# Eight adjacent output rows, zero-padded stationary slices, one store and filler matmuls in a decode kernel

## The chip, the cores and the metric

The kernel runs on one core of a Trainium2 chip. The metric is the device time of one execution in microseconds (us), given as the median of several executions. The profile's span is about 2 us shorter than that time (before: 110.88 us of span in an execution of 112.67 us), so differences are compared within one kind, never across. Engines are PE (matrix multiply), PEld (its weight loads), DVE (vector), ACT (scalar), POOL and SP. Most of the loads, and one store of the kernel before, are issued by SP; a few by ACT.

## The reference, cut to what matters

One token per batch row (2 rows, D = 448) is normalized. It goes through an attention over the last 2048 cache positions (16 query heads, 8 cached heads, head size 256) and the output product with wo, and separately through a two-layer block with w1 and w2. The two results are multiplied and added to x:

```python
xn = _layernorm(x, axis=-1)
s = _A_ref(xn, A_k_cache, A_v_cache, A_wq, A_wo)     # (2,1,4096) @ wo (4096,448) at its end
g = _silu(_B_ref(xn, B_w1, B_w2))                     # relu(xn@w1) @ w2 (1792,448)
return x + s * g
```

## The kernel before

44.11 MB of cache and weights are loaded for an output of 2 x 448 numbers. The attention is cut into four units u (batch x half of the cached heads). For each, K is transposed on PE, scores, softmax and the product with V follow. Apart from the load of x, the change touches only the end: the w2 product (`do_F`), the turn of the attention result into stationary form (`at2`, the operand that the weight loads bring into PE), the wo product and the store; around the last values product (`do_PV(3)`) it adds matmuls. wo arrives in five loads of 12, 12, 4, 2 and 2 row blocks of 128 rows each.

Both end products are held as four column groups i of 112 columns. Each matmul of a group of four writes its own 32-column strip of the PE array (`tile_position=(0, 32*i)`), so row b of group i stands in partition 32*i + b: eight useful rows, spread over 128 partitions.

```python
# x, loaded in the same layout (4 rows, 32 partitions apart, for each b)
d_xc = [pr.dma(ACTE, view(x_c, 0, [[1, NCOL]], n=4, p0=b, pstep=32),
               A_x[b, 0, :].rearrange("(i n) -> i n", i=4), [p_xc]) for b in range(B)]
...
# do_F: the w2 product; 14 row blocks x 4 column groups
for f in range(14):
    for i in range(4):
        lo = W2_AT + f * D + i * NCOL
        o = pr.op(PE, mm(view(fbk, 0, [[1, NCOL]], n=B, p0=32 * i), h_sb[:, 2 * f:2 * f + 2],
                         w2_sb[:, lo:lo + NCOL], f == 0, f == 13, tile_position=(0, 32 * i)), deps)
...  # exp, add, reciprocal, multiply: g_sb, 128 x 112
# the end of the program
do_F()
do_PV(3)
attend_scale(3)
attend_turn(3)
for b in range(2):
    ...  # two small matmuls and copies: at2, 128 x 64
for j in range(32):
    deps = deps + [landed.get(j)]            # the load that brought row block j
    for i in range(4):
        lo = j * D + i * NCOL
        m_o = pr.op(PE, mm(obk[32 * i:32 * i + B, 0:NCOL], at2[:, 2 * j:2 * j + 2],
                           wo_sb[:, lo:lo + NCOL], j == 0, j == 31, tile_position=(0, 32 * i)), deps)
        deps = []
v_t = ...   # tmp = obk * g_sb       128 x 112
v_o = ...   # out_sb = tmp + x_c     128 x 112
d_o = [pr.dma((SP, ACTE)[b], out[b, 0, :].rearrange("(i n) -> i n", i=4),
              view(out_sb, 0, [[1, NCOL]], n=4, p0=b, pstep=32), [v_o]) for b in range(B)]
```

## Time and profile before

| | before |
|---|---|
| median of executions | 112.84 us (112.78 to 112.84) |
| span of the profiled execution | 110.88 us |
| last wo load landed | 107.46 us |
| last wo matmul ended | 107.86 us |
| last vector operation ended | 108.49 us |
| from there to the end (the "tail" below) | 2.39 us |

These are rows of the page of the kernel before. The first three cut the span in 40 slices of 2.77 us: tenths of PE's time, tenths of full clock that PE was granted, tenths of the DMA engines' time. (The trace's record of the clock begins at 19.24 us; the nines before that are no measurement.) The last is the chain of waits, followed back from the last instruction, by engine.

```profile
PE   0010299995428999859999949699985464293480
PEclk9999999999995589995899995799999985555555
DMA  3988979898899889889989998998999999999920
...
DMA 56%; PE 34%; DVE 4%; SPq 2%; issue 1%; ACT 1%
```

The DMA row is full almost to the end, and the chain is mostly loads: the kernel is bound by bringing in its bytes. The end of the chain, in order of time (start, us, what), says what remains after the last byte.

```profile
83.07 24.39 DMA kbuf<-in_A_wo_dram
107.46 0.04 issue
107.50 0.39 PE obk L265 x8
...
107.91 0.28 DVE tmp L513
...
108.22 0.27 DVE out_sb L515
```

PE waits for the last load, does only the last eight of 128 wo matmuls after it, and two vector operations follow. The timeline of the kernel before shows how the wo matmuls run and how the stores are issued (start, duration, engine, line, operation, count).

```profile
102.38 1.29 PE L265 MATMUL obk<-kbuf,at 128*2 128x112 bf16 x48 [0.29 <-DVE at L502]
...
108.22 0.27 DVE L515 TENSOR_TENSOR out_sb<-tmp,x_c 128x112 bf16<-128x112 f32 x1
108.52 0.66 SPq L36 DMA_DIRECT2D out_dram<-out_sb  x1
108.52 0.56 ACTq L36 DMA_DIRECT2D out_dram<-out_sb  x1
```

48 matmuls in 1.29 us are 27 ns each, although PE runs at half clock. In the trace, the four of a row block start 1 to 6 ns apart, mostly 3 or 4, and the next four 93 ns later: four at a time, as the Trainium skill ("TensorE: Matmul & The Clock Gate", Part 3) says of tiles in different column groups.

The windows view of the kernel before, cut on the grid of the clock's changes (window, its length, then PE busy, PEld, DVE, ACT, POOL, clock, DMA share, GB/s), shows where the clock fell and how busy PE was then.

```profile
87.50:90.92 3.42, 2.11 (x70) 1.52 (x62) 1.51 (x5) 0.00 (x0) 0.00 (x0) 1.00 1.07 461
90.92:94.33 3.41, 1.55 (x64) 1.24 (x56) 1.26 (x3) 0.26 (x1) 0.00 (x0) 0.50 0.91 392
94.33:97.74 3.41, 1.39 (x16) 0.55 (x20) 0.27 (x1) 0.00 (x0) 0.00 (x0) 0.50 1.00 414
97.74:101.16 3.42, 2.47 (x28) 0.57 (x16) 0.81 (x2) 0.00 (x0) 0.00 (x0) 0.50 1.02 430
```

After a window in which PE was busy 2.11 of 3.42 us, the clock fell, and none of the later windows, of up to 2.47 busy us, was followed by a rise. The changes of the clock lie multiples of 3.41 us apart in the whole trace, which agrees with Part 1 of the same page: a free-running window of about 3.4 us.

### The profile page before, as it was taken

To read this page: it belongs to the slowest core of one execution; us is meant where nothing else is said; L and a number is where in the kernel's file an instruction comes from. 1 tells how busy PE (TensorE), PEld (TensorE's weight loads), DVE (VectorE), ACT (ScalarE), POOL (GpSimd) and SP (SyncE) were. 2 spreads that over 40 slices of the span, in tenths; PEclk is the share of its full clock that TensorE was granted. 3 is DMA by queue.
4 is the path that set the end of the run, shared out by engine and by line. 5 is a ranking of instruction groups with operands and counts; after the bars stand their busy time and mean duration, and the time that the engine had idled before them with its cause. 6 is when DMAs were issued, how large, how long until landed. Compare 5 with 4: busy or idle time off the path is not lost.

```text
span 110.9 us, 1921 instructions
## 1 busy us (share of the span) xinstructions
PE 74.0 (67%) x845; PEld 49.7 (45%) x845; DVE 48.0 (43%) x110; ACT 35.4 (32%) x43; POOL 1.9 (2%) x11
## 2 busy tenths in 40 slices
PE   0010299995428999859999949699985464293480
PEld 0000299952127977413777513397632244022350
DVE  2182042953433356553775653477546333104001
ACT  1960036760020647602286602076820200000000
POOL 6000000000000000000000000000000000000000
PEclk9999999999995589995899995799999985555555
DMA  3988979898899889889989998998999999999920
GB/s 95 473 379 379 520 331 496 355 567 372 378 532 414 378 378 556 384 378 532 417 366 390 526 402 378 520 426 378 387 382 416 454 434 423 408 426 427 394 98 1
DMA packets 2619, 44.22 MB, mean 399 GB/s; under 512 B 306, under 2 KB 564, under 8 KB 948
## 3 DMA queue, kind: packets, MB, share of 16 engines
q1 hardware_dynamic: 2584, 44.11, 93.5%
q8 instruction: 6, 0.10, 0.3%
q10 hardware_dynamic: 28, 0.00, 0.0%
q14 instruction: 1, 0.01, 0.0%
HBM read 44.11 MB, written 0.00 MB: 398 GB/s over the span
## 4 chain that ended last, share of the span: by engine, by line
DMA 56%; PE 34%; DVE 4%; SPq 2%; issue 1%; ACT 1%
DMA kbuf<-in_A_k_cache_dram 34%; PE tb L285 25%; DMA kbuf<-in_A_wo_dram 22%; PE sbk L265 5%; PE obk L265 2%; SPq L36 2%; PE mbk L265 1%; DVE s_sb L335 1%; ACT e_sb L340 1%; DVE rm L318 1%; DVE q_n L399 1%; PE mbk L345 1%; DVE pt L350 0%; DVE qz L409 0%; PE mbk L403 0%
## 5 line engine op out<-in xcount | busy, mean ns | idle before, releaser
L285 PE MATMUL tb<-ident_f,kbuf 128*128 128x128 f32 x256 | 36.6, 306 | 6.3 <-DMA kbuf<-in_A_k_cache_dram 6.3
L285 PEld LDWEIGHTS tb<-ident_f,kbuf 128*128 128x128 f32 x256 | 33.5, 161 | 10.4 <-DMA kbuf<-in_A_k_cache_dram 6.4
L295 ACT ACTIVATE kt<-tb 128x1024 bf16<-128x1024 bf16 x28 | 27.4, 1023 | 26.2 <-PE tb L285 26.2
L293 DVE COPY kt<-tb 128x1024 bf16<-128x1024 bf16 x36 | 24.7, 690 | 21.7 <-PE tb L285 21.7
L265 PE MATMUL obk<-vbuf,pt 128*16 128x512 bf16 x128 | 13.5, 529 | 3.5 <-DMA vbuf<-in_A_v_cache_dram 3.5
L265 PE MATMUL sbk<-kt,qz 128*32 128x512 bf16 x128 | 11.0, 393 | 1.7 <-DVE kt L293 1.1
L340 ACT ACTIVATE e_sb<-s_sb 128x512 bf16<-128x512 f32 x4 | 2.5, 630 | 22.9 <-DVE s_sb L335 22.9
L265 PEld LDWEIGHTS obk<-vbuf,pt 128*16 128x16 bf16 x128 | 3.2, 101 | 8.2 <-DMA vbuf<-in_A_v_cache_dram 4.4
L265 PE MATMUL mbk<-ident,xg 2*128 2x2 bf16 x7 | 0.3, 163 | 7.4 <-DVE xg L237 7.4
L372 DVE TENSOR_SCALAR o_sb<-obk,rs 128x512 bf16<-128x512 f32 x4 | 2.9, 735 | 5.4 <-PE obk L265 5.4
L265 PEld LDWEIGHTS sbk<-kt,qz 128*32 128x32 bf16 x128 | 2.7, 94 | 5.5 <-DVE kt L293 2.1
L265 PE MATMUL obk<-kbuf,at 128*2 128x112 bf16 x128 | 3.7, 292 | 2.1 <-DMA kbuf<-in_A_wo_dram 1.8
L318 DVE TENSOR_REDUCE rm<-sbk 128x4 f32<-128x512 f32 x4 | 2.8, 691 | 4.3 <-PE sbk L265 4.3
L350 DVE COPY pt<-mbk 128x512 bf16<-128x512 bf16 x4 | 1.7, 424 | 5.6 <-PE mbk L345 5.6
L345 PE MATMUL mbk<-ident,e_sb 128*128 128x128 bf16 x16 | 2.2, 286 | 2.6 <-ACT e_sb L340 2.6
L265 PEld LDWEIGHTS obk<-kbuf,at 128*2 128x2 bf16 x128 | 2.6, 112 | 3.1 <-DMA kbuf<-in_A_wo_dram 2.6
L265 PEld LDWEIGHTS mbk<-ident,xg 2*128 2x128 bf16 x7 | 0.3, 101 | 7.4 <-DVE xg L237 7.4
L345 PEld LDWEIGHTS mbk<-ident,e_sb 128*128 128x128 bf16 x16 | 1.3, 122 | 5.0 <-ACT e_sb L340 5.0
L323 PE MATMUL mbk<-ident_f,rm 128*1 128x128 f32 x4 | 1.1, 270 | 3.4 <-DVE rm L321 3.4
L265 PE MATMUL mbk<-one_f,mall 1*128 1x1 f32 x8 | 1.6, 268 | 2.5 <-DVE mall L330 2.5
L335 DVE SCALAR_TENSOR_TENSOR s_sb<-sbk,bias,low 128x512 f32<-128x512 f32 x4 | 3.0, 751 | 0.1
L323 PEld LDWEIGHTS mbk<-ident_f,rm 128*1 128x1 f32 x4 | 0.3, 79 | 5.4 <-DVE rm L321 5.4
(68 smaller groups left out, 37.0 us busy)
## 6 DMA issues: line engine op xcount, KB each, us to landing
kbuf<-in_A_k_cache_dram SPq DMA_DIRECT2D x4, 4096.0 KB, 27.1
vbuf<-in_A_v_cache_dram SPq DMA_DIRECT2D x3, 4096.0 KB, 37.0
vbuf<-in_A_wq_dram SPq DMA_DIRECT2D x1, 3584.0 KB, 20.1
kbuf<-in_B_w_dram SPq DMA_DIRECT2D x2, 1568.0 KB, 23.6
vbuf<-in_A_v_cache_dram SPq DMA_DIRECT2D x1, 3072.0 KB, 25.8
kbuf<-in_A_wo_dram SPq DMA_DIRECT2D x2, 1344.0 KB, 22.2
vbuf<-in_A_v_cache_dram SPq DMA_DIRECT2D x1, 1024.0 KB, 27.7
kbuf<-in_A_wo_dram SPq DMA_DIRECT2D x1, 448.0 KB, 24.3
```

What stands on the lines that cost most here:

```text
L36: o = _Op(eng, lambda e: e.dma_start(dst, src), [d for d in deps if d is not None], True)
L265: return lambda e: e.matmul(out_ap, lhsT=lhsT, rhs=rhs, start=start, stop=stop, skip_group_check=True, **kw)
L285: o = pr.op(PE, lambda e, n=n, lo=lo: e.matmul(bank_f[:, n * 128:(n + 1) * 128], lhsT=src_f[:, lo:lo + 128], rhs=ident_f[:, :], start=True ...
L293: evac[n_th] = pr.op(DVE, lambda e: e.tensor_copy(dst[:, :], bank[:, :]), deps)
L295: evac[n_th] = pr.op(ACTE, lambda e: e.activation(dst[:, :], bank[:, :], ACT.Copy), deps)
L318: v = pr.op(DVE, lambda e: e.tensor_reduce(out=rm4[:, :], in_=view(sbk, 0, [[1, 4], [4, 128]]), axis=AX.X, op=ALU.max), [st["S", u]])
L323: m = st["rmT", u] = pr.op(PE, lambda e: e.matmul(mbk_ap(0, 128, 1), lhsT=rm[:, :], rhs=ident_f[:, :], start=True, stop=True, is_transpose ...
L335: v = st["shift", u] = pr.op(DVE, lambda e: e.scalar_tensor_tensor(out=view(s_sb, 0, [[4, 128], [1, 4]]), in0=view(sbk, 0, [[4, 128], [1, ...
L340: a = st["exp", u] = pr.op(ACTE, lambda e: e.activation(e_sb[:, :], s_sb[:, :], ACT.Exp, accum_out=ssum[:, 0:1]), [v, st.get(("Pt", u - 1) ...
L345: o = pr.op(PE, lambda e, j=j: e.matmul(mb16[:, 512 + 128 * j:640 + 128 * j], lhsT=e_sb[:, 128 * j:128 * j + 128], rhs=ident[:, :], start= ...
L350: v = st["pt", u] = pr.op(DVE, lambda e: e.tensor_copy(view(pt[u % 2], 0, [[256, 2], [16, 16], [8, 2], [1, 8]]), view(mb16, 512, [[256, 2] ...
L372: st["osb", u] = st["obk"] = pr.op(DVE, lambda e: e.tensor_scalar(out=o_sb[:, :], in0=obk[:, :], scalar1=rs[:, u:u + 1], scalar2=None, op0 ...
```

## The change

The eight useful rows of the output, of the gate and of x are to stand in eight adjacent partitions (row 4*b + i), so that one store suffices. All four matmuls of a row block now write the same eight rows. To make matmul i touch only rows i and 4 + i, its stationary operand is an eight-column slice, out of an array with two useful columns and zeros around them (11 columns per row block, slice shifted by i). The sums of the other rows get zeros added. Matmuls without use ("fillers", four, two and one of 512 columns) are to keep PE's clock up. The whole diff:

```diff
--- before.py
+++ after.py
@@ -105,6 +105,8 @@
     FC = DFF // 2
     WO_PARTS = [12, 12, 4, 2, 2]
     NCOL = D // 4
+    NROW = 4 * B
+    GAP = NROW + 3
     NTB = 5
     ON_ACT = (1, 3, 5, 8, 10, 12, 14)
     FAR = -1.0e30
@@ -146,12 +148,12 @@
         q_n = named("q_n", [128, 512], BF)
         qz = named("qz", [128, 2 * NU * 64], BF)
         h_n = named("h_n", [128, FC // 4], BF)
-        h_sb = named("h_sb", [128, 28], BF)
-        x_c = named("x_c", [128, NCOL], BF)
-        ea = named("ea", [128, NCOL], F32)
-        g_sb = named("g_sb", [128, NCOL], F32)
-        tmp = named("tmp", [128, NCOL], F32)
-        out_sb = named("out_sb", [128, NCOL], BF)
+        h_z = named("h_z", [128, 14 * GAP], BF)
+        x_c = named("x_c", [NROW, NCOL], BF)
+        ea = named("ea", [NROW, NCOL], F32)
+        g_sb = named("g_sb", [NROW, NCOL], F32)
+        tmp = named("tmp", [NROW, NCOL], F32)
+        out_sb = named("out_sb", [NROW, NCOL], BF)
         rm4 = named("rm4", [128, 4], F32)
         rmm = named("rmm", [128, 4], F32)
         rm = named("rm", [128, 1], F32)
@@ -165,7 +167,7 @@
         pt = [named(f"pt{i}", [128, 512], BF) for i in range(2)]
         o_sb = named("o_sb", [128, 512], BF)
         at_exp = named("at_exp", [128, 256], BF)
-        at2 = named("at2", [128, 64], BF)
+        at_z = named("at_z", [128, 32 * GAP], BF)
         kbuf = [named(f"kbuf{i}", [128, UW], BF) for i in range(2)]
         vbuf = [named(f"vbuf{i}", [128, UW], BF) for i in range(2)]
         kt = [named(f"kt{i}", [128, 1024], BF) for i in range(NCHUNK)]
@@ -184,9 +186,7 @@
             return cache[b, 4 * v:4 * v + 4, SK - W:SK, :].rearrange("h (r t) d -> r h (t d)", t=NT)
 
         d_x = pr.dma(ACTE, x_sb[0:B, :], A_x[:, 0, :])
-        p_xc = pr.op(POOL, lambda e: e.memset(x_c[:, :], 0.0))
-        d_xc = [pr.dma(ACTE, view(x_c, 0, [[1, NCOL]], n=4, p0=b, pstep=32),
-                       A_x[b, 0, :].rearrange("(i n) -> i n", i=4), [p_xc]) for b in range(B)]
+        d_xc = pr.dma(ACTE, x_c[:, :], A_x[:, 0, :].rearrange("b (i n) -> (b i) n", i=4))
 
         wq_sb, w1_sb, w2_sb, wo_sb = vbuf[1], kbuf[0], kbuf[0], kbuf[1]
         W2_AT = SLOTS * FC
@@ -223,6 +223,7 @@
             base=0, pattern=[[-1, 128]], channel_multiplier=1), [i1])
         p_one = pr.op(POOL, lambda e: e.memset(one_f[:, :], 1.0), [p_idf])
         p_qz = pr.op(POOL, lambda e: e.memset(qz[:, :], 0.0), [p_one])
+        p_z = [pr.op(POOL, lambda e, t=t: e.memset(t[:, :], 0.0)) for t in (h_z, at_z)][-1]
 
         a_z = [pr.op(ACTE, lambda e, t=t: e.memzero(t[:, :])) for t in (obk,)][-1]
 
@@ -430,7 +431,7 @@
                                      ident[:, 32 * i:32 * i + 4], j == 0, tile_position=(0, 32 * i)), deps)
                     deps = []
             st["hT"] = pr.op(DVE, lambda e: e.tensor_copy(
-                view(h_sb, 0, [[2, 7], [14, 2], [1, 2]]), view(hbk, 0, [[4, 7], [2, 2], [1, 2]])), [o])
+                view(h_z, 3, [[GAP, 7], [7 * GAP, 2], [4, 2]]), view(hbk, 0, [[4, 7], [2, 2], [1, 2]])), [o, p_z])
 
         def do_F():
             fbk = tb[1][:, :].bitcast(F32).tensor
@@ -438,16 +439,23 @@
             for f in range(14):
                 for i in range(4):
                     lo = W2_AT + f * D + i * NCOL
-                    o = pr.op(PE, mm(view(fbk, 0, [[1, NCOL]], n=B, p0=32 * i), h_sb[:, 2 * f:2 * f + 2], w2_sb[:, lo:lo + NCOL],
-                                     f == 0, f == 13, tile_position=(0, 32 * i)), deps)
+                    o = pr.op(PE, mm(view(fbk, 0, [[1, NCOL]], n=NROW), h_z[:, f * GAP + 3 - i:f * GAP + 3 - i + NROW],
+                                     w2_sb[:, lo:lo + NCOL], f == 0 and i == 0, f == 13 and i == 3), deps)
                     deps = []
-            f_ap = view(fbk, 0, [[1, NCOL]])
+            f_ap = view(fbk, 0, [[1, NCOL]], n=NROW)
             a_e = pr.op(ACTE, lambda e: e.activation(ea[:, :], f_ap, ACT.Exp, scale=-1.0), [o])
             v_d = pr.op(DVE, lambda e: e.tensor_scalar(
                 out=ea[:, :], in0=ea[:, :], scalar1=1.0, scalar2=None, op0=ALU.add), [a_e])
             v_rc = pr.op(DVE, lambda e: e.reciprocal(tmp[:, :], ea[:, :]), [v_d])
             st["g"] = pr.op(DVE, lambda e: e.tensor_tensor(
                 out=g_sb[:, :], in0=f_ap, in1=tmp[:, :], op=ALU.mult), [v_rc])
+
+        def idle_work(n):
+            wbk = tb[2][:, :].bitcast(F32).tensor
+            deps = [evac[NU * NCHUNK - 2], v_fold]
+            for _ in range(n):
+                pr.op(PE, mm(view(wbk, 0, [[1, 512]]), ident[:, :], kt[0][:, 0:512], True, True), deps)
+                deps = []
 
         def scores(u):
             for i in range(NCHUNK):
@@ -493,30 +501,32 @@
         attend_turn(2)
         do_hT()
         do_F()
+        idle_work(4)
         do_PV(3)
         attend_scale(3)
+        idle_work(2)
         attend_turn(3)
+        idle_work(1)
         for b in range(2):
             m_at = pr.op(PE, mm(mbk_ap(256 + 32 * b, 32), at_exp[:, 128 * b:128 * b + 128],
                                 fold[:, :], True, True), [st["at", NU - 1], v_fold, st["mbk"]])
             v_at2 = st["mbk"] = pr.op(DVE, lambda e, b=b: e.tensor_copy(
-                view(at2, b, [[2, 32]]), mbk_ap(256 + 32 * b, 32)), [m_at])
+                view(at_z, 3 + 4 * b, [[GAP, 32]]), mbk_ap(256 + 32 * b, 32)), [m_at, p_z])
         deps = [v_at2, st["obk"]]
         landed = dict(d_wo)
         for j in range(32):
             deps = deps + [landed.get(j)]
             for i in range(4):
                 lo = j * D + i * NCOL
-                m_o = pr.op(PE, mm(obk[32 * i:32 * i + B, 0:NCOL], at2[:, 2 * j:2 * j + 2], wo_sb[:, lo:lo + NCOL],
-                                   j == 0, j == 31, tile_position=(0, 32 * i)), deps)
+                m_o = pr.op(PE, mm(obk[0:NROW, 0:NCOL], at_z[:, j * GAP + 3 - i:j * GAP + 3 - i + NROW],
+                                   wo_sb[:, lo:lo + NCOL], j == 0 and i == 0, j == 31 and i == 3), deps)
                 deps = []
         v_t = pr.op(DVE, lambda e: e.tensor_tensor(
-            out=tmp[:, :], in0=obk[:, 0:NCOL], in1=g_sb[:, :], op=ALU.mult), [m_o, st["g"]])
+            out=tmp[:, :], in0=obk[0:NROW, 0:NCOL], in1=g_sb[:, :], op=ALU.mult), [m_o, st["g"]])
         v_o = pr.op(DVE, lambda e: e.tensor_tensor(
-            out=out_sb[:, :], in0=tmp[:, :], in1=x_c[:, :], op=ALU.add), [v_t, *d_xc])
-        d_o = [pr.dma((SP, ACTE)[b], out[b, 0, :].rearrange("(i n) -> i n", i=4),
-                      view(out_sb, 0, [[1, NCOL]], n=4, p0=b, pstep=32), [v_o]) for b in range(B)]
-        pr.op(SP, None, d_o)
+            out=out_sb[:, :], in0=tmp[:, :], in1=x_c[:, :], op=ALU.add), [v_t, d_xc])
+        d_o = pr.dma(ACTE, out[:, 0, :].rearrange("b (i n) -> (b i) n", i=4), out_sb[:, :], [v_o])
+        pr.op(ACTE, None, [d_o])
 
         with nc.Block() as block:
             pr.run(block)
```

## The prediction

> **What bounds it.** The page shows DMA at about 90% in nearly every slice, 44.11 MB at 398 GB/s; the chain of waits is 56% DMA and ends in the load of wo. Landings: wo parts (12, 12, 4, 2, 2 row blocks) at 102.0, 105.24, 106.34, 106.90 and 107.46 us. Nothing in the change issues these loads earlier, so only the tail after 107.46 can move: 8 matmuls to 107.86, two vector operations to 108.49, stores to the end at 110.88.
>
> **PE cost.** Before, the four 112-column matmuls of a row block sit in four column groups and start 3-4 ns apart (single starts in the timeline); a group of four takes 93 ns at clock 0.5, so 128 cost 3.0 us of issue. The Trainium skill, "TensorE: Matmul & The Clock Gate", Part 3, says such tiles run concurrently; the trace agrees. In the change all four write the same eight partitions, so they go one after another. Serial 128-column bf16 transposes step 56 ns at clock 1.0 and 107 ns at 0.5; scaled to 112 columns I estimate 49 and 93 ns. The wo product becomes 6.3 us warm or 11.9 us cold; w2's 56 matmuls go from 1.3 us to 2.7 or 5.2 us.
>
> On the critical path: 80 of the 128 wo matmuls cannot start before 105.24. Warm they start until about 109.15 and end near 109.4, against 107.86: +1.5 us. The w2 product and the first 48 fit in idle time if the clock is warm.
>
> **Clock.** Before, it falls to 0.5 at 90.92 and stays there. The windows view and the clock record show changes only on a 3.41 us grid (49.96 down, 53.37 up, 67.03 down, 70.44 up, 90.92 down); windows with PE busy throughout raised it, 83% did not, about 55-62% let it fall. The same page, Part 1, has this free-running window; the trace agrees. In the change w2 (5.2 us cold from 91.38), four fillers (427 ns each cold) and the last values product are dense for over 6.8 us, so a full window must fall in it: I expect clock 1.0 by 98.2 at the latest. Risk: a warm PE waits for the last v part (98.74) and for DVE, a window of perhaps 50-60% busy; the fillers may not hold it. A fall at 101.2 would cost about 1.7 us more.
>
> **Store.** Both stores are issued at 108.52; ACT's completes at 110.13, SP's at 110.48. One store on ACT saves about 0.35 us. The start (one x load fewer, one memset moved) is off the path: the first K load lands at 13.08. DVE and ACT operations over 8 partitions cost what 128 cost.
>
> **Sum.** 112.84 + 1.5 - 0.35 = 114.0 warm; about 115.7 if the clock falls again; about 121 if it stays 0.5 (serial wo from 104.4 to 116.4). Weighted towards the first: 114.3 us, 113.4 to 117.5 in 8 of 10. Faster by over 2%: 0.03; within: 0.58; slower: 0.39.
>
> **What would show it.** Starts of wo matmuls 49 ns apart rather than groups of four; wo landings unchanged within 0.2 us; the chain ending in PE obk work of 3.9 us or more after the second wo part, instead of waiting on the last; clock 1.0 from 94-98 us; one store, last operation to end about 2.05 us instead of 2.4.
>
> **What would make it wrong.** Narrow 8-column matmuls not counting as busy, so that the clock stays 0.5; weight loads of odd-aligned 8-column slices not hiding; fillers delaying the values product while cold; loads landing later.

## The result, and the profile after

Every ratio in this text is the mean time of one kernel's fast executions over that of the other's of the same rounds, so it is not quite the ratio of the medians quoted. An execution counts as slow, and is left out of ratios, when it is over 1.5% above the fastest of its kernel.

| | before | after |
|---|---|---|
| median of executions | 112.81 us (112.70 to 112.84) | 113.71 us (113.54 to 113.99) |
| ratio, 95% interval | | 1.0084 (1.0061 to 1.0107) |
| span of the profiled execution | 110.88 | 112.00 |
| w2 product, first start to last end | 91.38 to 92.85 | 92.73 to 97.89 |
| last values product | 96.35 to 99.94 | 98.80 to 100.70 |
| wo product | 102.38 to 107.86 | 103.30 to 109.76 |
| last wo load landed | 107.46 | 107.52 |
| tail after the last vector operation | 2.39 | 1.65 |

The change makes the kernel about 0.8% slower (1.3% in later rounds, under "The changed kernel once more"). The same rows of the page after, and its two largest changed groups (busy us, mean ns, idle before):

```profile
PE   0010299986328999859999859599955678995991
PEclk9999999999985599985999995999999555599999
DMA  3988979998998898899899899899799999999800
...
PE 51%; DMA 34%; DVE 10%; issue 2%; ACT 1%
...
L266 PE MATMUL obk<-kbuf,at_z 128*8 128x112 bf16 x128 | 6.5, 213 | 0.4 <-DVE at_z L513 0.4
...
L266 PE MATMUL tb<-kbuf,h_z 128*8 128x112 bf16 x56 | 5.2, 293 | 0.4 <-DVE h_z L433 0.4
```

DMA has left the end of the chain: its share fell from 56% to 34%, and PE's rose from 34% to 51%. The chain after, in order of time, has no load after 71.72 us.

```profile
91.74 0.57 PE tb L266 x28
...
92.73 5.17 PE tb L266 x56
97.89 0.16 issue
98.06 0.81 PE tb L266 x3
98.87 1.86 PE obk L266 x32
...
103.30 6.47 PE obk L266 x128
109.80 0.27 DVE tmp L524
110.09 0.26 DVE out_sb L526
```

The 128 wo matmuls start 49.2 ns apart, one after the other at full clock, and fill 6.47 us without a gap. The loads had all landed 2.2 us before they ended. Ahead of them stands the w2 product at 93 ns a matmul, then fillers (three of the four left a record), then the values product; the last two V loads had landed at 96.35 and 98.80. The timeline's end shows the store:

```profile
110.09 0.26 DVE L526 TENSOR_TENSOR out_sb<-tmp,x_c 8x112 bf16<-8x112 f32 x1
110.39 0.30 ACTq L36 DMA_DIRECT2D out_dram<-out_sb  x1
```

One issue takes 0.30 us where the two before took 0.56 and 0.66. And this is the windows view after, on the grid of this execution:

```profile
90.69:94.11 3.42, 2.68 (x60) 2.15 (x53) 0.77 (x3) 0.00 (x0) 0.00 (x0) 0.50 0.94 402
94.11:97.52 3.41, 3.41 (x39) 3.41 (x38) 0.00 (x0) 0.00 (x0) 0.00 (x0) 0.50 0.98 402
97.52:100.93 3.41, 3.25 (x44) 1.34 (x42) 1.48 (x4) 0.25 (x1) 0.00 (x0) 1.00 1.02 428
100.93:104.35 3.42, 2.23 (x31) 1.43 (x30) 1.40 (x4) 0.00 (x0) 0.00 (x0) 1.00 0.99 411
```

The window 94.11 to 97.52 is full, with nothing but the narrow eight-column w2 matmuls, and the clock rises at its end, before the first filler starts at 98.06. It then stays up.

So two sums stand against each other in the profiled executions: the wo product ends 1.90 us later (109.76 against 107.86), and the tail is 0.74 us shorter. The span grew by 1.12 us, which is what is left after small differences in the vector operations. One pair of profiles is one draw, though: the w2 product started 1.35 us later (92.73 against 91.38), and the change did little of that: the clock fell one window earlier (at 87.28 against 90.92), which made the matmuls ahead of it slow. In the run without fillers below, whose kernel is otherwise the changed one, it started at 91.36. The experiments ask what each of the two sums consists of.

### The profile page after: what moved, and what is told of

Its sections match the earlier page's. It is cut to its first block, busy times and chain, and to the rows that moved or that the text cites. A ratio compares the mean times of both kernels' runs of the same rounds, so it can differ in the third digit from the quotient of the medians.

```text
span 112.0 us, 1933 instructions
## 1 busy us (share of the span) xinstructions
PE 81.1 (72%) x851; PEld 57.6 (51%) x852; DVE 48.3 (43%) x110; ACT 35.3 (32%) x43; POOL 2.3 (2%) x12
## 4 chain that ended last, share of the span: by engine, by line
PE 51%; DMA 34%; DVE 10%; issue 2%; ACT 1%
DMA kbuf<-in_A_k_cache_dram 34%; PE tb L286 25%; PE obk L266 11%; PE tb L266 6%; PE sbk L266 5%; PE mbk L266 2%; DVE s_sb L336 1%; ACT e_sb L341 1%; DVE o_sb L373 1%; DVE rm L319 1%; PE mbk L346 1%; DVE q_n L400 1%; DVE kt L294 1%; DVE at_z L513 1%; DVE mrow L327 1%
## 5 line engine op out<-in xcount | busy, mean ns | idle before, releaser
L266 PE MATMUL obk<-vbuf,pt 128*16 128x512 bf16 x128 | 12.1, 479 | 0.0
L266 PE MATMUL obk<-kbuf,at_z 128*8 128x112 bf16 x128 | 6.5, 213 | 0.4 <-DVE at_z L513 0.4
L266 PEld LDWEIGHTS obk<-kbuf,at_z 128*8 128x8 bf16 x128 | 6.3, 87 | 0.5 <-DVE at_z L513 0.5
L266 PE MATMUL tb<-kbuf,h_z 128*8 128x112 bf16 x56 | 5.2, 293 | 0.4 <-DVE h_z L433 0.4
L266 PEld LDWEIGHTS tb<-kbuf,h_z 128*8 128x8 bf16 x56 | 5.0, 127 | 0.5 <-issue 0.5
```

Source lines behind the costliest of these rows:

```text
L266: return lambda e: e.matmul(out_ap, lhsT=lhsT, rhs=rhs, start=start, stop=stop, skip_group_check=True, **kw)
```

## The experiments

All runs were timed against the kernel before on the same chip. "WRONG on purpose" marks kernels whose output is not meant to be right. The product s * g is at most 0.0004 here, far under x, so the comparison with the reference passes even one of those; it says little about the end of these kernels. Runs of different batches were on different chips; each batch had its own rounds of the kernel before.

### Two stores again

```diff
-d_o = pr.dma(ACTE, out[:, 0, :].rearrange("b (i n) -> (b i) n", i=4), out_sb[:, :], [v_o])
+d_o = [pr.dma((SP, ACTE)[b], out[b, 0, :].rearrange("(i n) -> i n", i=4),
+              out_sb[4 * b:4 * b + 4, :], [v_o]) for b in range(B)]
```

> The changed kernel with its one store split again into two (rows 0-3 from SP, rows 4-7 from ACT). In the traces the last vector operation to the end of the span took 2.36 us before and 1.6 us after. Theory (the single store itself is the gain): the tail after the last vector operation goes back to about 2.3 us, and the time rises by about 0.7 us to 114.4 us. Rival (the tail shortened because of the adjacent partitions or the end barrier, not the number of stores): stays at 113.7 us.

Measured: 113.94 us (113.64 to 115.19), ratio to before 1.0116 (1.0075 to 1.0157). The tail is 1.79 us, not 2.3. The theory that the single store is the gain falls: going from two stores to one is worth 0.14 us of the tail (1.79 against 1.65). The timeline shows two side-by-side issues that are nevertheless quick:

```profile
110.20 0.35 SPq L36 DMA_DIRECT2D out_dram<-out_sb  x1
110.20 0.28 ACTq L36 DMA_DIRECT2D out_dram<-out_sb  x1
```

### Both stores of the kernel before on ACT

```diff
-d_o = [pr.dma((SP, ACTE)[b], out[b, 0, :].rearrange("(i n) -> i n", i=4),
+d_o = [pr.dma(ACTE, out[b, 0, :].rearrange("(i n) -> i n", i=4),
...
-pr.op(SP, None, d_o)
+pr.op(ACTE, None, d_o)
```

> The kernel before with both stores issued one after the other by ACT, nothing else. Before, the two issues run side by side and take 0.56 (ACT) and 0.66 us (SP); the single 8-row issue after took 0.30 us. Theory (two queues issuing together slow each other): each issue takes about 0.3 us here, the second store lands about 0.3 us after a single one would, the tail is about 1.9 us instead of 2.36 and the time about 112.4 us. Rival (a 4-row issue costs 0.55 us whoever else issues): 0.55 us each, the tail 2.2 to 2.4 us, the time 112.7 to 112.9 us.

Measured: 113.37 us (113.23 to 113.52), ratio 1.0043 (1.0030 to 1.0056). The timeline shows the two issues as one entry:

```profile
108.68 1.14 ACTq L36 DMA_DIRECT2D out_dram<-out_sb  x2
```

They took 0.56 and 0.54 us with nobody else issuing, so the theory of two queues that slow each other falls. The rival had the issue right and the time wrong: it overlooked that the second issue now waits for the first, which made the tail 2.69 us. What the slow stores have in common, here and before, is that the four rows lie 32 partitions apart.

### Adjacent rows in the kernel before (WRONG on purpose)

```diff
-view(out_sb, 0, [[1, NCOL]], n=4, p0=b, pstep=32)
+view(out_sb, 0, [[1, NCOL]], n=4, p0=4 * b)
```

> WRONG RESULT ON PURPOSE: the kernel before, its two stores from SP and ACT reading four adjacent partitions each (0-3 and 4-7) instead of partitions 32 apart; nothing else differs. Theory (the 32-partition step of the stored tile is what makes an issue slow, 0.56 and 0.66 us against 0.28 and 0.35 in the changed kernel with two stores): both issues take about 0.3 us, the tail after the last vector operation falls from 2.39 to about 1.8 us, the time to about 112.3 us. Rival (something else of the changed kernel makes its stores quick): tail 2.4 us, 112.9 us.

Measured: 112.14 us (111.97 to 112.28), ratio 0.9935 (0.9922 to 0.9947). The output was wrong, as meant. The tail is 1.78 us. The timeline:

```profile
108.31 0.28 DVE L515 TENSOR_TENSOR out_sb<-tmp,x_c 128x112 bf16<-128x112 f32 x1
108.61 0.35 SPq L36 DMA_DIRECT2D out_dram<-out_sb  x1
108.61 0.28 ACTq L36 DMA_DIRECT2D out_dram<-out_sb  x1
```

The partition step alone, with the same two queues, byte counts and destinations, takes 0.61 us out of the tail (2.39 to 1.78). In the trace the first descriptor (one row's transfer) of the ACT store starts 0.77 us after the issue began (109.38 against 108.61), and 1.20 us with the step of 32 (109.72 against 108.52). The SP store, which completes last and so ends the kernel, gains more: 0.79 us against 1.56 (108.52 to 110.08). So of the 0.74 us that the changed store saves, 0.61 are adjacency and about 0.13 the one store fewer. Only the steps 1 and 32 were run.

### The wo product of the changed kernel in column groups (WRONG on purpose)

```diff
-mm(obk[0:NROW, 0:NCOL], at_z[...], wo_sb[...], j == 0 and i == 0, j == 31 and i == 3)
+mm(obk[32 * i:32 * i + NROW, 0:NCOL], at_z[...], wo_sb[...], j == 0, j == 31, tile_position=(0, 32 * i))
```

> WRONG RESULT ON PURPOSE: the changed kernel, but the 128 wo matmuls write four column groups (eight partitions at 0, 32, 64, 96) as before, so they overlap in fours, and only the first group is used. Store, fillers, w2 product stay as changed. Theory (the serial wo product is what costs): PE waits for the last wo part again (about 107.5), the last matmul ends near 107.8, the single store still saves 0.75 us, so the time is about 112.0 us, under both kernels. Rival (late start of the wo product, from the cold w2 product and the fillers, is what costs): little change, above 113.2 us.

Measured: 112.06 us (111.95 to 112.24), ratio 0.9930 (0.9917 to 0.9942), under both kernels as the theory said. The chain ends in the last load again:

```profile
85.24 22.34 DMA kbuf<-in_A_wo_dram
107.58 0.04 issue
107.62 0.30 PE obk L266 x8
107.92 0.02 issue
107.95 0.27 DVE tmp L524
```

It does so although the wo product began as late as 103.44 in this execution. With four matmuls at a time a late start is caught up while the loads still come in; with one at a time it is not. The serial order of the wo product, with all that it exposes, is the loss: 113.71 against 112.06 us, 1.65 us by the medians (taken in different rounds, in which before had 112.81 and 112.89). The w2 product stayed serial here; what its order adds to the late start was not run by itself.

### No fillers, and only the last three

```diff
-idle_work(4)      # between the w2 and the values product; a_fill3 removes only this one
 do_PV(3)
 attend_scale(3)
-idle_work(2)
 attend_turn(3)
-idle_work(1)
```

> The changed kernel without its seven filler matmuls. In the changed kernel's trace the clock rose at 97.52, before the first filler began at 98.06, so the dense w2 product raised it alone. Theory (fillers only delay): the values product starts about 0.8 us earlier, the wo product about 0.8 us earlier, and the time falls to about 113.2 us. Rival (fillers hold the clock up through the sparse stretch after the values product): the clock falls to 0.5 near 101, part of the wo product runs at 93 ns a matmul, and the time rises by 1.5 us or more to 115.3 us.

> The changed kernel without the first four fillers, with the three later ones. Theory (the first four only delay the values product by up to 0.8 us; the later three hold the clock): 113.2 to 113.6 us with little spread. Rival (all seven are needed): as without any, 113.6 to 116 us, with falls of the clock near 101 in the trace.

Without fillers: 114.34 us (113.61 to 116.05; the last is marked slow), ratio 1.0122 (1.0081 to 1.0163). In the profiled execution, a fast one of 115.31 us, the windows view shows the rival's case:

```profile
97.58:101.00 3.42, 1.16 (x17) 0.37 (x13) 0.97 (x2) 0.00 (x0) 0.00 (x0) 1.00 1.03 431
101.00:104.41 3.41, 2.51 (x28) 2.43 (x28) 0.60 (x2) 0.00 (x0) 0.00 (x0) 0.50 0.98 407
104.41:107.82 3.41, 3.41 (x40) 3.41 (x38) 0.00 (x0) 0.00 (x0) 0.00 (x0) 0.50 0.48 179
```

PE is busy 1.16 of 3.42 us while it waits for the last V load and for DVE, the clock falls at 101.00, and most of the wo product runs at half pace until 107.82. The product takes 9.14 us (102.12 to 111.26). Two other executions of the same kernel took 113.6 us, about the changed kernel's time; none reached the 113.2 of the first theory. All six profiles of kernels with a serial w2 product and at least the last three fillers keep the clock at full from its rise in the w2 product (or before) to the end of the wo product, so it is likely that the fillers take away this fall. That they make the kernel quicker on the whole is not shown: without them the fast executions took 113.61 to 115.31 us, with them 113.41 to 115.07 in later rounds (below), and the intervals of the ratios overlap.

With the last three fillers only: 113.79 us (113.60 to 114.18), ratio 1.0081 (1.0063 to 1.0099), which is the changed kernel's 113.71 again, and a little over the theory's range. As the theory said, the profile has no fall of the clock near 101. The profiled wo product started at 102.25, a whole microsecond earlier than in the changed kernel's profile, and ended at 109.54, only 0.22 us earlier. Its chain says why:

```profile
83.33 22.07 DMA kbuf<-in_A_wo_dram
105.40 0.04 issue
105.44 4.11 PE obk L266 x80
```

80 of the 128 matmuls wait for the second wo load, and 80 at 49 ns are 3.9 us. The end is the later of two bounds: the start plus 6.47 us, or the second load plus about 4.1 us.

### The clock up all the way, and wo in smaller parts

```diff
-WO_PARTS = [12, 12, 4, 2, 2]
+WO_PARTS = [8, 4, 4, 4, 4, 4, 2, 2]
...
-softmax(3, values(2))
+softmax(3, [lambda: (do_PV(2, (0,)), idle_work(3)), lambda: idle_work(1),
+            lambda: (do_PV(2, (1, 2)), idle_work(4)), lambda: do_PV(2, (3,))])
+idle_work(4)
...
-idle_work(4)
-do_PV(3)
+idle_work(8)
+do_PV(3, (0, 1, 2))
+idle_work(4)
+do_PV(3, (3,))
```

> The changed kernel with more fillers, so that the clock is 1.0 from the last softmax on (12 in the last softmax, 8 and 4 round the values product), and wo in eight parts of 8, 4, 4, 4, 4, 4, 2, 2 row blocks. Theory (the serial wo product is bound by its own 6.3 us and by its start, which the cold w2 product and the fillers put at 103.3): the w2 product takes 2.8 us, the wo product starts at about 102.1 and ends at about 108.5, the time is about 112.6 us. Rival (the start does not matter, because the second wo part or the last parts bound the end): stays at 113.5 us or above.

Measured: six executions, in two groups: 112.62 to 112.67 us (four) and 114.03 and 114.04 (two). The ratio is 1.0016 (0.9973 to 1.0060), which decides nothing. The larger group is where the theory put it, 1.1 us under the changed kernel's first rounds. The edit changed the fillers and the parts of wo together, so it does not tell which of the two gains this. The profile fell in the slower group. There the w2 product ran at full clock (2.91 us), but began at 93.28, and the wo product at 103.53. The clock had been at half from 72.44 to 75.85, in the middle of the last unit's K transposes, which made that unit's softmax and all after it late; the fillers themselves held PE from 96.35 to 98.02 and from 99.42 to 100.39. That the quicker group had its low windows elsewhere is argued only: there is no profile of it.

### Fillers in the kernel before

The edit is the three `idle_work` lines of the change, and its helper, put into the kernel before.

> The kernel before with the seven fillers alone. Theory (before waits for the last wo part whatever the clock, so fillers gain nothing): 112.7 to 112.9 us; if they raise the clock, the last eight matmuls end at most 0.1 us sooner. Rival (a warmer clock at the end is worth something by itself): under 112.5 us.

Measured: 112.81 us (112.69 to 112.96), ratio 0.9991 (0.9978 to 1.0004). The fillers gain nothing here. In the profiled execution they did not keep the clock up to the end: it was full from 96.21 to 103.04 and at half after that, so this run says nothing of a full clock at the end. That is in the trace of a_tiled_wrong (the wo product in column groups, above), where the last eight matmuls took 0.30 us on the chain instead of 0.39. In the profile of this run, too, the clock was low during the last K transposes, and the w2 product began at 93.18; the kernel absorbed it (112.96 us).

### The changed kernel once more

> The changed kernel once more, for the spread of its time over the phase of the clock windows: theory (the clock may fall during the last softmax or later, depending on where the 3.41 us grid lies; the serial wo product is exposed to a late start), 113.5 to 114.3 us with executions of higher mean clock among the quicker ones; the kernel before, which waits for the last load, stays within 0.3 us. Rival (no such exposure): as narrow as before.

Measured: 113.41, 113.84, 115.01 and 115.07 us, and two executions marked slow; ratio 1.0130 (1.0082 to 1.0179). The kernel before took 112.73 to 113.03 us in the same rounds. The upper end is above what was expected. The spread of 1.7 us is within the fast executions alone, against 0.3 us for the kernel before. The part of the expectation that a higher mean clock goes with a quicker execution is not clean: the quickest had 0.924, and the next three 0.893 to 0.895 with times 1.2 us apart. The mean says how often the clock was low, not where.

The profile fell in one of the two executions marked slow (115.33 us; the 1.5% line runs through the group of 115.01 to 115.36). Its chain shows where the time was lost:

```profile
104.82 6.47 PE obk L266 x128
```

The wo product takes the same 6.47 us as in the first profile but starts 1.52 us later (104.82 against 103.30), and the execution took 1.53 us longer (115.33 against 113.80). The clock was at half from 71.67 to 75.08, in the last K transposes, and everything after them is late by 1.5 to 1.6 us up to the end. No fast execution near 115 us was profiled; that 115.01 and 115.07 have the same cause is likely, not shown.

### A version that keeps both gains

The kernel before keeps its column groups. Its product with the gate is written as bf16, and one matmul with a 128 x 8 matrix of zeros and ones moves the eight rows together:

```diff
+v_sel = pr.op(DVE, lambda e: e.tensor_copy(view(sel, 0, [[4, B], [1, 4]]), view(ident, 0, [[1, B], [32, 4]])))
...
-out=tmp[:, :], in0=obk[:, 0:NCOL], in1=g_sb[:, :], op=ALU.mult
+out=sg[:, :], in0=obk[:, 0:NCOL], in1=g_sb[:, :], op=ALU.mult
+m_r = pr.op(PE, mm(view(rbk, 0, [[1, NCOL]], n=8), sel[:, :], sg[:, :], True, True), [v_t, evac[NU * NCHUNK - 1]])
-out=out_sb[:, :], in0=tmp[:, :], in1=x_c[:, :], op=ALU.add
+out=out_sb[:, :], in0=view(rbk, 0, [[1, NCOL]], n=8), in1=x_c[:, :], op=ALU.add
-d_o = ...two stores...
+d_o = pr.dma(ACTE, out[:, 0, :].rearrange("b (i n) -> (b i) n", i=4), out_sb[:, :], [v_o])
```

x is loaded into eight adjacent rows as in the change, and the bank of the w2 product is zeroed first, so that unused rows cannot bring infinities into the sum. No fillers.

> A version meant to keep both gains: the kernel before with its four column groups for w2 and wo, then one extra matmul with a 128x8 selection matrix moves the product with the gate from partitions 32i+b to eight adjacent ones, and x and the one store are as in the changed kernel; no fillers. Theory (adjacent rows save about 0.74 us of the store, serial matmuls cost 1.65 us, a single dependent matmul about 0.3 us with its waits): last wo matmul near 107.9, tail after the last vector operation 1.65 us, time 112.4 us. Rival (the adjacent store only pays in the changed kernel's surroundings): 112.8 us or more.

Measured: 112.44 us (112.34 to 112.69), ratio 0.9958 (0.9945 to 0.9971): under both kernels, and where the sum put it. The profiled execution is the slowest of the five (112.69 us); its last wo load landed at 107.91, and its last wo matmul ended at 108.31, later than expected. The timeline:

```profile
108.36 0.27 DVE L516 TENSOR_TENSOR sg<-obk,g_sb 128x112 bf16<-128x112 f32 x1 [6.02 <-PE obk L267]
108.68 0.26 PE L267 MATMUL tb<-sg,sel 128*8 128x112 bf16 x1 [0.38 <-DVE sg L516]
108.98 0.26 DVE L521 TENSOR_TENSOR out_sb<-tb,x_c 8x112 bf16<-8x112 f32 x1 [0.35 <-PE tb L267]
109.27 0.30 ACTq L36 DMA_DIRECT2D out_dram<-out_sb  x1
```

The extra step costs 0.35 us between the two vector operations (0.04 before), and the tail is 1.65 us. Because the comparison with the reference can hardly see s * g, the eight rows of the product were also compared in a simulation of both kernels: they differ by at most 9.2e-7, with a largest value of 4.3e-4, which is the rounding to bf16. (In a repeat, the product s * g stored as bf16 was the same number for number in the kernel before, the changed one and this one.)

## Why the prediction was right

The total was right: 113.71 us against 114.3 us, within the range, and "within 2%". Point by point:

- **What bounds the kernel.** Right. The wo loads landed at the same times within 0.1 us (107.52 against 107.46), so what the change adds comes after them. Vector and scalar operations over 8 partitions cost what 128 cost, as it said (0.26 against 0.27 us for the last addition).
- **Serial matmuls.** Right. The estimate of 49 ns was scaled from transposes of 128 columns; the trace has 49.2 ns. Column groups restored (a_tiled_wrong), the loss went.
- **The end of the wo product, "+1.5 us".** Right in mechanism, too small in the profiled execution: +1.90 us. The step that failed is "the w2 product and the first 48 fit in idle time if the clock is warm". The w2 product ran cold for all but its last few matmuls (92.73 to 97.89), the fillers held PE until the values product at 98.80, and wo started at 103.30 rather than by 102.4. PE never waited for the second wo load, which the text had made the bound; a_fill3 shows that bound, and the changed kernel its own start plus 6.47 us. The other profiles of the serial product end it at 109.54 to 111.28, so the forecast of 109.4 is the floor, and +1.90 is one draw. How much of the late start is the serial w2 product, the fillers or the earlier fall of the clock was not separated.
- **The clock.** Right that a full window must fall in the dense stretch: it rose at 97.52 (forecast: by 98.2). It also was right that a fall near 101 was a danger: a_nofill shows it at 101.00, with 115.31 us, which is 1.7 over that kernel's best executions (of which there is no profile), the 1.7 that the text named. In the profiles of the changed kernel the clock stays up. What the text did not foresee is a fall earlier, in the K transposes, as in the profile of after_again. Its shares of busy time were read off coarsely: on the grid, the window that did not raise the clock was busy for 85% of its time (32.89 to 36.31), and those that let it fall for 20 to 62%.
- **The store, "saves about 0.35 us".** The mis-sized term: 0.74 us. The text gave the gain to one store in place of two. The runs give 0.13 us to that and 0.61 us to the adjacent partitions (b_adjacent_wrong), which shorten both the issue and the time to the first descriptor. The trace before had a hint: the two loads of x into rows 32 apart took 0.58 and 0.51 us to issue (one load into eight adjacent rows takes 0.28 in the trace after).
- **The sum.** In the profiles the two errors (0.40 us too little loss, 0.39 us too little gain) cancel. The median lands 0.3 us under the "warm" figure of 114.0; that figure was right partly by luck.
- **The range.** It holds the later rounds too (113.41 to 115.36 us), and it was wide for a reason that the runs support: where the clock falls differs between executions, and a serial product at the end is exposed to that.

## What to carry to other kernels

Before packing a result into fewer rows, count what the packing does to the matmuls that run after the last load: four concurrent column groups became one stream of 6.47 us, which ended 2.2 us after the last load where the groups had ended 0.4 us after it. Rows that lie in adjacent partitions can be quicker to store than rows 32 apart (0.61 us of the tail here), and one selecting matmul (0.35 us here) can bring rows together after the concurrent products. A kernel that ends by waiting for a load hides what the PE clock does before that (the kernel before took 112.71 to 113.05 us over the later rounds); one that ends in PE work shows it as spread between executions (113.41 to 115.07 us in fast ones).

## What the Trainium skill lacked or had wrong

- "DMA: Bandwidth & Descriptors", Rules for kernel authors and Latency and other measured facts: nothing on what the partition step of a small store costs. Here four rows of 224 bytes took 0.56 us (ACT) and 0.66 us (SP) to issue with rows 32 partitions apart, and 0.28 and 0.35 us with adjacent rows; the first descriptor started 1.20 us (ACT) and 1.56 us (SP) after the issue began, and 0.77 and 0.79 us with adjacent rows. Why, no run here shows. The step is not all: the first load of x, two adjacent rows of 896 bytes and the first transfer on ACT's queue, took 0.55 us to issue.
- "TensorE: Matmul & The Clock Gate", Part 1: no threshold for a "busy" window. The profile's busy time gives none either: windows with 2.70 of 3.41 us (b_fill, 92.80 to 96.21) and 2.96 of 3.41 us (without fillers, 90.76 to 94.17) raised the clock, and windows with 2.90 of 3.42 us (before, 32.89 to 36.31) and 3.16 of 3.42 us (b_one_queue, 66.11 to 69.53) did not; a window of 2.11 us let it fall before, and one of 2.04 us (84.09 to 87.50) did not. So the profile's busy time alone does not decide. Matmuls with eight stationary columns count as busy (rise at 97.52 after a window of nothing else).
- The same page, Part 4, says that the full clock does not engage for matmuls in transpose mode. In the trace before, a window of nothing but fp32 transposes (36.31 to 39.72) ended in a rise of the clock at 39.72. Here the measurement decides.
- The same page's advice to keep PE warm does not say when it gains nothing: seven fillers in the kernel before, whose end waits for a load, gave a ratio of 0.9991 (0.9978 to 1.0004).
